# 906 more elements of a value block kept in PSUM, gate weights in two loads, one score product moved: a decode kernel that streams 218 MB

## The chip, the cores and the metric

The kernel runs on one core of a Trainium2 chip. The metric is the device time of one execution in microseconds (us). The profile's span, from the first to the last instruction, is about 1.4 us shorter than that time.

Engines are named as in the profile: PE is TensorE, PEld its weight loads, DVE VectorE, ACT ScalarE, POOL GpSimd, SP SyncE. SP issues nearly all loads, in one queue; 16 DMA engines carry them out. A "packet" is one row of one load as the trace records it: a load for 128 partitions has 128 packets, 8 for each DMA engine, and each packet has a start, a duration and a size.

## The reference, cut to what matters

One token goes twice through an attention layer and a gated MLP, with the same weights and the same caches both times.

```python
def _A_ref(x, k_cache, v_cache, wq, wo):      # 32 heads of 192, window of the last 4096 keys
    q = (x @ wq).reshape(B, Sq, Hq, Dh).transpose(0, 2, 1, 3)
    k = k_cache[:, :, Sk - W:, :]; v = v_cache[:, :, Sk - W:, :]
    p = softmax(einsum("bhqd,bhkd->bhqk", q, k) * Dh ** -0.5)
    return einsum("bhqk,bhkd->bhqd", p, v).transpose(...).reshape(B, Sq, Hq * Dh) @ wo

def _B_ref(x, w_gate, w_up, w_down):          # 640 -> 1536 -> 640
    return (sigmoid(x @ w_gate) * (x @ w_up)) @ w_down

x = A_x
x = x + _A_ref(layernorm(x), ...);  x = x + _B_ref(layernorm(x), ...)     # layer 0
x = x + _A_ref(layernorm(x), ...);  x = x + _B_ref(layernorm(x), ...)     # layer 1
```

(Transposes and shapes are abbreviated.) Each number of a cache or weight is used once per layer, so the work is moving them. What layer 0 leaves on the chip need not be loaded again in layer 1.

## The kernel before: the parts that matter

The heads are handled as 16 pairs. A pair has an "a" block (query weights and keys) and a "b" block (values and output weights), each 14208 bf16 elements per partition; SBUF has seven such slots and one region of 12288 elements, `mreg`, in cells of `FW` = 640. Pairs 0, 14 and 15 stay in their slots from layer 0 to layer 1. While the MLP weights of layer 0 stream through `mreg`, part of pair 1's values waits in PSUM banks that nobody uses then. DVE copies it in, 32 bits at a time ("stow"), and out again in layer 1:

```python
NST = 3 * FW // 2
stash = [(bank[i][:, c:c + n].bitcast(U32), 2 * n)
         for i, c, n in ((3, 0, NST // 2), (6, 0, NST // 2), (7, DC, 512 - DC))]
NSV = sum(n for _, n in stash)                 # 960 + 960 + 1014 = 2934 bf16 elements
...
# loads of the MLP weights into mreg: name -> (first cell, first block, last block)
MW = {"wg0": (0, 0, 3), "wg1": (3, 3, 6), "wg2": (6, 6, 9), "wg3": (9, 9, 12), "u0": (12, 0, 2), "u1": (14, 2, 7),
      "d0": (0, 0, 3), "d1": (3, 3, 6), "u2": (6, 7, 10), "u3": (9, 10, 12), "d2": (11, 6, 9), "d3": (14, 9, 12)}
MAFTER = {"d0": ("wg0",), "d1": ("wg1",), "u2": ("wg2",), ...}      # a load waits for the products that free its cells
# loads of the rest of pair 1's values: name -> (first cell, last cell)
MV = {"v1": (17, len(rc)), "v0": (NSV // FW, 6), "v2": (6, 11), "v3": (11, 14), "v4": (14, 17)}
VAFTER = {"v1": "u1", "v0": "d1", "v2": "u3", "v3": "d2", "v4": "d3"}
```

Here "wg", "u" and "d" are gate, up and down weights. "The gate weights of layer 1" means the gate weights that are loaded in this stage, at the passage from layer 0 to layer 1. The attention of layer 1 starts so:

```python
mark("a14_0", Q(14, 0))                        # query of pair 14; mark() lets loads be issued
mark("QM", Q(PM, 1, 5))                        # PM = 1: query of pair 1
ln_sq(xi)
mark("a14_1", QK(14, 0, ks=(0,)))              # scores of pair 14
mark("a14_2", QK(14, 0, ks=(1, 2)))
...
soft(1, hook=lambda: Q(2, None))               # softmax statistics of pair 15
for i in (2, 0, 1):
    ...                                        # the three copies from PSUM back to mreg
expo(1)                                        # exponential of pair 15
QK(0, 0)                                       # scores of pair 0, which free a slot
soft(0, mid=lambda: PVmm(14, 0))
```

Of the kernel before, what the change touches and what calls it, by code (L numbers as in the profile page):

```python
# [8 lines left out]
U32 = mybir.dt.uint32  # L9
# [9 lines left out]
DC, FC = D // P, F // P  # L19
# [90 lines left out]
def decode_kernel(ctx: ExitStack, nc, cx: bass.AP, uc: bass.AP,  # L110
# [52 lines left out]
    bank += [o8_ps[:, 0:512], o8_ps[:, 512:1024]] + [ctx.enter_context(nc.psum_tensor(f"bank{i}", [P, 512], FP32)) for i in (6, 7)]  # L163
    qe, dmx, oT3 = bank[2][:, 0:P], bank[2][:, P:2 * P], bank[2][:, 2 * P:2 * P + 3]
    o8, yT = bank[4:6], bank[7]
    stash = [(bank[i][:, c:c + n].bitcast(U32), 2 * n) for i, c, n in ((3, 0, NST // 2), (6, 0, NST // 2), (7, DC, 512 - DC))]
    NSV = sum(n for _, n in stash)

    def words(v, out, in_):
        return v.tensor_scalar(out=out.bitcast(U32), in0=in_.bitcast(U32), scalar1=0, scalar2=None, op0=ALU.bitwise_or)  # L170
# [4 lines left out]
    def res(name):  # L175
        if name not in R:
# [4 lines left out]
    rval = [res(f"val{i}") for i in range(NSLOT)]  # L181
    rc = [res(f"cell{i}") for i in range(-(-ME // FW))]
    MW = {"wg0": (0, 0, 3), "wg1": (3, 3, 6), "wg2": (6, 6, 9), "wg3": (9, 9, 12), "u0": (12, 0, 2), "u1": (14, 2, 7),
          "d0": (0, 0, 3), "d1": (3, 3, 6), "u2": (6, 7, 10), "u3": (9, 10, 12), "d2": (11, 6, 9), "d3": (14, 9, 12)}
    MAFTER = {"d0": ("wg0",), "d1": ("wg1",), "u2": ("wg2",), "u3": ("wg3",), "d2": ("wg3", "u0"), "d3": ("u1",)}
    MV = {"v1": (17, len(rc)), "v0": (NSV // FW, 6), "v2": (6, 11), "v3": (11, 14), "v4": (14, 17)}
    VAFTER = {"v1": "u1", "v0": "d1", "v2": "u3", "v3": "d2", "v4": "d3"}

    PLACE = {s: i for i, s in enumerate((0, 3, 2, 1, 4, 5, 6))}

# [36 lines left out]
    def last_values(l, p):  # L227
        return [("b1", l, p), ("b0", l, p)]
    seq = [("a", 0, 0)] + [("c", 0, p) for p in range(1, 15)] + [("a", 0, 15), ("b", 0, 14)] + last_values(0, 15)
    seq += [("wol", 14), ("wol", 15)] + [(k,) for k in (*MW, "v1", "wq2", "v0", "v2", "v3", "v4", "wq3", "wom")] + [("a0", 1), ("a0", 2), ("a", 1, 3), ("b", 1, 2)]  # L230
    seq += [("b", 1, 3), ("a", 1, 4), ("b", 1, 4), ("a", 1, 5), ("a", 1, 6), ("b", 1, 5)]
    seq += [("c", 1, p) for p in range(7, 13)] + [("a", 1, 13), ("b", 1, 12)] + last_values(1, 13)
    seq += [("fg",), ("fu",), *(("fd", i) for i in range(len(WFIN)))]
# [18 lines left out]
    def try_load(it):  # L252
        k = it[0]
        if k == "c":
            l, p = it[1:]
            ss = A_SLOT[l][p], B_SLOT[l][p - 1]
            if any(x in busy for x in ss):
                return False
            busy.update(ss)
            first = min(ss, key=PLACE.get)  # L260
            assert abs(PLACE[ss[0]] - PLACE[ss[1]]) == 1 and first == ss[p % 2]
            pg.dma(q_dma(slot(first, 0, 2 * UNIT), uc[p]), f"c{l}{p % 2}", wr=[rslot[x] for x in ss])
            values_in(ss[1])
        elif k == "a":
            s = A_SLOT[it[1]][it[2]]
            if not take(s):
                return False
            o0 = WQE if it[1:] == (1, 3) else 0
            pg.dma(q_dma(slot(s, o0, UNIT - o0), a_in(it[2], o0)), f"c{it[1]}{it[2] % 2}" if it[1:] in ((0, 15), (1, 4), (1, 5), (1, 6), (1, 13)) else f"a{it[1]}_{it[2]}", wr=[rslot[s]])
        elif k == "b":  # L270
            s = B_SLOT[it[1]][it[2]]
            if not take(s):
                return False
            o0, n0 = WOE if it[1:] == (0, 14) else 0, len(pg.ops["dma"])
            pg.dma(q_dma(slot(s, o0, UNIT - o0), b_in(it[2], o0)), f"b{it[1]}_{it[2]}", wr=[rslot[s]])
            if it[1:] == (0, 14):
                ev_done["b14"] = list(pg.ops["dma"][n0]["deps"].items())
            values_in(s)
        elif k == "b1":
            s = B_SLOT[it[1]][it[2]]  # L280
            if not take(s):
                return False
            n, o1 = len(pg.ops["dma"]), UNIT if it[1] else VE
            pg.dma(q_dma(slot(s, NHALF, o1 - NHALF), b_in(it[2], NHALF, o1)), f"b1_{it[1]}", wr=[rslot[s]])
            ev_done["b1"] = list(pg.ops["dma"][n]["deps"].items())
        elif k == "b0":
            s = B_SLOT[it[1]][it[2]]
            pg.dma(q_dma(slot(s, 0, NHALF), b_in(it[2], 0, NHALF)), "bh0", wr=[res("bh0")], extra=ev_done["b1"])
        elif k == "a0":
            if f"a14_{it[1]}" not in ev_done:  # L290
                return False
            s = A_SLOT[1][2]
            o0, o1 = ((WQE, A0CUT), (A0CUT, UNIT))[it[1] - 1]
            pg.dma(q_dma(slot(s, o0, o1 - o0), a_in(2, o0, o1)), f"a0{it[1]}", wr=[res(f"a0{it[1]}")] + ([rslot[s]] if it[1] == 2 else []),
                   extra=[ev_done[f"a14_{it[1]}"]])
        elif k == "wol":
            s = B_SLOT[0][it[1]]
            o = wo_at(it[1])
            pg.dma(q_dma(slot(s, o, WOE), b_in(it[1], o, o + WOE)), f"wol{it[1]}", wr=[res(f"wol{it[1]}")], extra=ev_done["b1" if it[1] == 15 else "b14"])
        elif k in MW:  # L300
            if any("done_" + n not in ev_done for n in MAFTER.get(k, ())):
                return False
            c, f0, f1 = MW[k]
            src = {"w": wg_d, "u": wu_d, "d": wd_d}[k[0]]
            pg.dma(q_dma(mreg(c * FW, (f1 - f0) * FW), src[:, f0 * FW:f1 * FW]), k, wr=rc[c:c + f1 - f0])
        elif k in MV:
            if "done_" + VAFTER[k] not in ev_done:
                return False
            c0, c1 = MV[k]
            o0, o1 = max(c0 * FW, NSV), min(c1 * FW, ME)  # L310
            pg.dma(q_dma(mreg(o0, o1 - o0), b_in(PM, o0, o1)), k, wr=rc[c0:-(-o1 // FW)])
        elif k == "wq2":
            if "done_d0" not in ev_done:
                return False
            pg.dma(q_dma(mreg(0, WQE), a_in(2, 0, WQE)), k, wr=rc[0:WQE // FW])
        elif k == "wq3":
            if "a14_0" not in ev_done:
                return False
            pg.dma(q_dma(slot(A_SLOT[1][2], 0, WQE), a_in(3, 0, WQE)), k, wr=[res(k)], extra=[ev_done["a14_0"]])
        elif k == "wom":  # L320
            if "QM" not in ev_done:
                return False
            pg.dma(q_dma(slot(A_SLOT[1][PM], 0, WOE), b_in(PM, VE, UNIT)), "wom", wr=[res("wom")], extra=[ev_done["QM"]])
        elif k == "fg":
            pg.dma(q_dma(mreg(0, 12 * FW), wg_d), "fg", wr=rc)
        elif k == "fu":
            if not take(U_SLOT):
                return False
            pg.dma(q_dma(slot(U_SLOT, 0, 12 * FW), wu_d), "fu", wr=[rslot[U_SLOT]])
        else:  # L330
            if it[1] == 0 and not take(D_SLOT):
                return False
            c0, c1 = WFIN[it[1]]
            pg.dma(q_dma(slot(D_SLOT, c0 * D, (c1 - c0) * D), wdp(c0, c1)), f"wf{it[1]}", wr=[rslot[D_SLOT]] if it[1] == 0 else [])
        return True
# [55 lines left out]
    def attention(l, xi):  # L391
# [42 lines left out]
                release(sa)  # L434
            return ev

        def soft(x=0, hook=None, mid=None):
            sc_x = S[x]
            pg.op("dve", lambda v: v.reduce_max(out=mx, in_=sc_x[0][:], axis=AX.X), wr=[res("mx")], ex=sc_x[3:5])  # L439
            if hook is not None:  # L440
# [2 lines left out]
            if mid is not None:  # L443
                mid()
            pg.op("pe", lambda t: t.matmul(dmx[:, 0:P], lhsT=ones_f, rhs=diag[:], start=True, stop=True), rd=[res("diag"), res("ones")], ex=[rb[2]])  # L445
            pg.op("dve", lambda v: v.tensor_reduce(out=nb2, in_=dmx[:, 0:P].rearrange("p (a r) -> p r a", r=2), axis=AX.X, op=ALU.max, negate=True),  # L446
                  wr=[res("nb2")], ex=[rb[2]])
            pg.op("dve", lambda v: v.tensor_tensor_reduce(out=nbj, in0=nb2, in1=pm_s, scale=1.0, scalar=0.0, op0=ALU.mult, op1=ALU.add, accum_out=nbias),  # L448
                  rd=[res("nb2"), res("pm_s")], wr=[res("nbj"), res("nbias")], multi=True)

# [14 lines left out]
                  rd=[res("rowsum"), res("wsel")], wr=[res(f"rs2{z}")])  # L465

        def RS(z, bk=4):
            sm = bank[bk][:, 2 * DH:2 * DH + 2]
            pg.op("pe", lambda t: t.matmul(sm, lhsT=ones_f, rhs=rs2[z], start=True, stop=True), rd=[res(f"rs2{z}"), res("ones")], wr=[res("rsum")], ex=[rb[bk]])  # L469
            for h in range(2):  # L470
                rb[bk].last["dve"] = pg.op("dve", lambda v, h=h: v.reciprocal(out=Rn[z][64 * h:64 * h + 64], in_=sm[64 * h:64 * h + 64, h:h + 1]),  # L471
# [83 lines left out]
        def step(p, prev):  # L555
# [1 line left out]
                ev = PVn(prev - 1, 1 - prev % 2)  # L557
            Q(p, 0)
            QK(p, 0)
            soft(0)  # L560
            if (l, prev) == (0, PM):
                stow(2, [ev])
            expo()
# [13 lines left out]
        def loop(p0, n):  # L577
            for it in range(n // 2):
                pg.seg = (l, it)
                for p in (p0 + 2 * it, p0 + 2 * it + 1):  # L580
                    step(p + 1, p)
                    if (l, p) == (0, PM):
                        stow(0)
                        stow(1)
            pg.seg = None
        if l == 0:
            Q(0, 0)
# [14 lines left out]
        else:  # L602
            mark("a14_0", Q(14, 0))
            mark("QM", Q(PM, 1, 5))
            ln_sq(xi)
            mark("a14_1", QK(14, 0, ks=(0,)))
            mark("a14_2", QK(14, 0, ks=(1, 2)))
# [4 lines left out]
            expo()  # L612
            ET(0)
            Q(0, 0)
            soft(1, hook=lambda: Q(2, None))
            for i in (2, 0, 1):
                o, n = sum(m for _, m in stash[:i]), stash[i][1]
                pg.op("dve", lambda v, i=i, o=o, n=n: words(v, mreg(o, n), stash[i][0]), rd=[res(f"stash{i}")], wr=rc[o // FW:-(-(o + n) // FW)],
                      ex=[rb[7]] if i == 2 else [], own="st")
            expo(1)  # L620
            QK(0, 0)
            soft(0, mid=lambda: PVmm(14, 0))
            PVout(14, 0)
            ET(1)
# [30 lines left out]
    def mlp(l, xi):  # L655
# [65 lines left out]
        for i in range(2):  # L721
            f0, f1 = HS[i], HS[i + 1]
            if i:
# [2 lines left out]
            pg.op("dve", lambda v, i=i, f0=f0, f1=f1: v.scalar_tensor_tensor(out=hT[:, f0:f1], in0=bank[ubank[i]][:, 0:f1 - f0], scalar=rstd_c,  # L726
                                                                            in1=eg[:, f0:f1], op0=ALU.mult, op1=ALU.mult),
                  rd=[res("rstd"), res("eg")], wr=[res(f"hT{i}")], ex=[rb[ubank[i]]])
        down("d2", "d3")
        return residual(xi)  # L730

    def finish():
# [213 lines left out]
```

## Time and profile before

| | before |
|---|---|
| time, median of 3 | 514.11 us (513.99 to 514.98) |
| span of the profiled execution | 512.7 us |
| bytes moved, mean rate | 218.71 MB, 427 GB/s |
| packet times of all queues, sum / 16 engines | 509.65 us |
| first packet, last landing of weights | 1.0 us, 510.2 us |

The first lines of the profile page of the kernel before: busy time and share for each engine, then slices (40 equal ones; a digit is a busy share in tenths), the rate in GB/s by slice, all packets, and the shares of the chain of waits that ended last.

```profile
span 512.7 us, 8580 instructions
...
PE 260.9 (51%) x3716; PEld 136.9 (27%) x3716; DVE 100.4 (20%) x379; ACT 84.8 (17%) x171; POOL 4.2 (1%) x31
...
DMA  9999999999999999999999999999999999999996
GB/s 426 430 423 426 427 430 428 426 435 448 439 430 426 440 430 430 426 435 457 399 422 416 418 440 436 435 430 427 443 443 443 430 426 426 440 431 417 431 427 275
DMA packets 9820, 218.71 MB, mean 427 GB/s; under 512 B 1224, under 2 KB 1608, under 8 KB 4808
...
DMA 63%; PE 23%; DVE 7%; ACT 3%; issue 2%; SPq 2%; DVEq 0%; POOL 0%; ACTq 0%; POOLq 0%
```

The row to read is DMA: 9 up to the last slice. No other engine is busy more than 51% of the time. The chain of waits gives DMA only 63%, which could tempt one to shorten the other 37%. But the chain follows one thread of waits through a steady flow; it doesn't say that the DMA engines rested while PE computed, and the DMA row says that they didn't, as far as slices of 12.8 us can. (A packet counts whole in the slice in which it starts. So single slices can show more than the mean rate, and shares in windows more than 1.)

How much the queue holds in reserve can be worked out: for each load, the last of its 16 completions in the trace, less the moment at which the next load is issued. I call this the *lead*. In the kernel before the smallest is 4.5 us. The 16 engines don't finish a load together (2 us apart in this stage), so the earliest engine's lead is smaller: the first of the 16 completions less the next issue, 2.5 us at least in this stage and 2.4 in the whole run.

The issue of loads between the layers, from SP's part of the timeline (start, duration, line, what is loaded, how many merged into the line):

```profile
259.99 1.86 SPq L214 DMA_DIRECT2D big<-in_wg_dram  x4
261.89 4.56 SPq L214 DMA_DIRECT2D big<-in_wu_dram  x2
275.25 0.90 SPq L214 DMA_DIRECT2D big<-in_wd_dram  x2
276.97 1.48 SPq L214 DMA_DIRECT2D big<-in_wu_dram  x2
```

The gate and up loads are in the queue 14 us ahead. From 275.25 us on, each load needs cells that the products have only just freed: here the queue is short.

The order of events around pair 0's scores (timeline; PE's scores L429, the copies out of PSUM L170, pair 15's exponential L453, and the next load):

```profile
301.29 2.75 PE L429 MATMUL scores<-big,qs 128*32 128x512 bf16 x24
...
301.83 1.94 DVE L170 TENSOR_SCALAR big<-bank 128x507 uint32<-128x507 uint32 x3
301.93 1.20 ACT L453 ACTIVATE e_sb<-o,sc 128x1024 bf16<-128x1024 f32 x1 [1.41 <-DVE sc L448]
...
304.09 0.33 SPq L214 DMA_DIRECT2D big<-in_uc_dram  x1
```

### The profile page before, as it was taken

The numbers are of one execution on the slowest core, as the hardware profiler recorded it, in microseconds if no ns is written. First come the engines' busy times: TensorE is split into PE (matmuls) and PEld (weight loads), VectorE is DVE, ScalarE is ACT, GpSimd is POOL, SyncE is SP. The second block draws the span as 40 slices with busy tenths as digits, with TensorE's granted clock in tenths as the row PEclk, the third lists the DMA queues.
The fourth block names the chain that finished last, engine by engine and source line by source line (L and its number), as shares of the span: only waits on it lengthen the run. The fifth ranks groups of instructions, "written<-read, shape, count | busy, mean of one in ns | idle before, by whom it ended". The sixth has DMA issues, their size and how long they took to land.

```text
span 512.7 us, 8580 instructions
## 1 busy us (share of the span) xinstructions
PE 260.9 (51%) x3716; PEld 136.9 (27%) x3716; DVE 100.4 (20%) x379; ACT 84.8 (17%) x171; POOL 4.2 (1%) x31
## 2 busy tenths in 40 slices
PE   0452456344634454326566767873625244634665
PEld 0221222122312221112234434432312122312334
DVE  0221221111210221112121243321202111210311
ACT  1110111011101111011121033130301011101220
POOL 0010000000000000000000000000000000000000
PEclk9995555566556566675575578665857556556675
DMA  9999999999999999999999999999999999999996
GB/s 426 430 423 426 427 430 428 426 435 448 439 430 426 440 430 430 426 435 457 399 422 416 418 440 436 435 430 427 443 443 443 430 426 426 440 431 417 431 427 275
DMA packets 9820, 218.71 MB, mean 427 GB/s; under 512 B 1224, under 2 KB 1608, under 8 KB 4808
## 3 DMA queue, kind: packets, MB, share of 16 engines
q1 hardware_dynamic: 9656, 218.37, 99.2%
q8 instruction: 13, 0.21, 0.1%
q10 hardware_dynamic: 144, 0.06, 0.0%
q14 instruction: 7, 0.06, 0.0%
HBM read 218.43 MB, written 0.00 MB: 426 GB/s over the span
## 4 chain that ended last, share of the span: by engine, by line
DMA 63%; PE 23%; DVE 7%; ACT 3%; issue 2%; SPq 2%; DVEq 0%; POOL 0%; ACTq 0%; POOLq 0%
DMA big<-in_uc_dram 54%; PE scores L429 9%; PE o L488 7%; DMA big<-in_wd_dram 6%; DMA big<-in_wu_dram 3%; DVE sc L439 3%; PE bank L445 2%; PE bank L411 2%; SPq L214 2%; ACT e_sb L453 2%; PE bank L523 1%; PE bank L459 1%; ACT diag L442 1%; DVE sc L471 1%; PE o L469 1%
## 5 line engine op out<-in xcount | busy, mean ns | idle before, releaser
L429 PE MATMUL scores<-big,qs 128*32 128x512 bf16 x744 | 83.6, 619 | 10.3 <-DVE qs L417 9.6
L411 PE MATMUL bank<-sh,big 128*128 128x1 bf16 x465 | 17.2, 166 | 133.3 <-DMA big<-in_uc_dram 130.9
L488 PE MATMUL o<-big,et_sb 128*2 128x384 bf16 x1024 | 76.1, 465 | 6.1 <-DMA big<-in_uc_dram 3.6
L442 ACT ACTIVATE diag<-cst,sc 128x128 f32<-128x128 bf16 x32 | 12.8, 401 | 310.2 <-DVE sc L439 299.3
L439 DVE TENSOR_REDUCE sc<-scores 128x1 f32<-128x1024 f32 x31 | 37.9, 1224 | 79.1 <-PE scores L429 79.1
L411 PEld LDWEIGHTS bank<-sh,big 128*128 128x128 bf16 x465 | 14.7, 104 | 136.5 <-DMA big<-in_uc_dram 113.2
L445 PE MATMUL bank<-diag,sc 128*128 128x128 f32 x64 | 21.8, 436 | 46.7 <-ACT diag L442 46.7
L453 ACT ACTIVATE e_sb<-scores,sc 128x1024 bf16<-128x1024 f32 x31 | 37.3, 1204 | 39.7 <-DVE sc L448 37.4
L417 DVE TENSOR_TENSOR qs<-bank,cst 128x96 bf16<-128x96 f32 x30 | 7.7, 258 | 163.6 <-PE bank L411 163.6
L488 PEld LDWEIGHTS o<-big,et_sb 128*2 128x2 bf16 x1024 | 27.8, 106 | 41.7 <-issue 28.6
L429 PEld LDWEIGHTS scores<-big,qs 128*32 128x32 bf16 x744 | 24.2, 134 | 45.0 <-issue 33.2
L495 ACT CAST o_sb<-o 128x384 bf16<-128x384 f32 x64 | 29.6, 474 | 21.4 <-PE o L488 21.3
L445 PEld LDWEIGHTS bank<-diag,sc 128*128 128x128 f32 x64 | 13.6, 265 | 71.5 <-ACT diag L442 70.5
L523 PE MATMUL bank<-sh,big 128*128 128x1 bf16 x480 | 17.3, 165 | 15.5 <-DVE sh L512 14.9
L463 DVE CAST et_sb<-bank 128x64 bf16<-128x64 f32 x32 | 7.2, 225 | 69.8 <-PE bank L459 69.8
L523 PEld LDWEIGHTS bank<-sh,big 128*128 128x128 bf16 x480 | 14.6, 99 | 18.0 <-DVE sh L512 12.4
L446 DVE TENSOR_REDUCE sc<-bank 128x2 f32<-128x128 f32 x32 | 9.3, 292 | 40.1 <-PE bank L445 40.1
L459 PE MATMUL bank<-cst,e_sb 128*128 128x8 bf16 x256 | 11.7, 169 | 7.8 <-ACT e_sb L453 7.6
L459 PEld LDWEIGHTS bank<-cst,e_sb 128*128 128x128 bf16 x256 | 9.0, 101 | 23.9 <-issue 17.4
L469 PE MATMUL o<-sc 128*128 128x2 f32 x62 | 13.8, 292 | 0.6 <-ACT o_sb L495 0.6
L469 PEld LDWEIGHTS o<-sc 128*128 128x128 f32 x62 | 11.9, 239 | 1.9 <-ACT o_sb L495 1.3
L471 DVE RECIPROCAL sc<-o 64x1 f32<-64x1 f32 x62 | 10.2, 164 | 10.0 <-PE o L469 8.2
(78 smaller groups left out, 105.9 us busy)
## 6 DMA issues: line engine op xcount, KB each, us to landing
big<-in_uc_dram SPq DMA_DIRECT2D x20, 7104.0 KB, 22.7
big<-in_uc_dram SPq DMA_DIRECT2D x11, 3552.0 KB, 21.4
big<-in_uc_dram SPq DMA_DIRECT2D x2, 3072.0 KB, 18.8
big<-in_uc_dram SPq DMA_DIRECT2D x7, 480.0 KB, 6.5
big<-in_uc_dram SPq DMA_DIRECT2D x1, 2784.0 KB, 12.3
big<-in_uc_dram SPq DMA_DIRECT2D x1, 2304.0 KB, 10.0
big<-in_uc_dram SPq DMA_DIRECT2D x1, 2048.0 KB, 11.7
big<-in_wg_dram SPq DMA_DIRECT2D x4, 480.0 KB, 15.1
```

The costliest lines, as they stand in the source:

```text
L411: ins = t.matmul(qe[:, i:i + 1], lhsT=w[:, c * 2 * DH + c0:c * 2 * DH + c0 + P], rhs=xq[:, c:c + 1], start=(c == 0), stop=(c == DC - 1))
L429: ins = t.matmul(sc_x[1 + b][32 * j:32 * j + 32, :], lhsT=qs[:, y, k, :], rhs=slot(sa, WQE + k * W + (4 * b + j) * 512, 512), start=(k == ...
L439: pg.op("dve", lambda v: v.reduce_max(out=mx, in_=sc_x[0][:], axis=AX.X), wr=[res("mx")], ex=sc_x[3:5])
L442: pg.op("act", lambda a: a.mul(out=diag[:], in_=ident, mul=mx), rd=[res("cst"), res("mx")], wr=[res("diag")])
L445: pg.op("pe", lambda t: t.matmul(dmx[:, 0:P], lhsT=ones_f, rhs=diag[:], start=True, stop=True), rd=[res("diag"), res("ones")], ex=[rb[2]])
L453: pg.op("act", lambda a: a.activation(out=e_sb[:], in_=sc_x[0][:], func=ACT.Exp, bias=nbias, scale=srs_c, accum_out=rowsum), rd=[res("nbia ...
L459: ins = t.matmul(qe[:, 0:2 * NB].rearrange("p (r x) -> p r x", r=2)[:, :, 4 * b:4 * b + 4], lhsT=e_sb[:, b * P:(b + 1) * P], rhs=sel, star ...
L469: pg.op("pe", lambda t: t.matmul(sm, lhsT=ones_f, rhs=rs2[z], start=True, stop=True), rd=[res(f"rs2{z}"), res("ones")], wr=[res("rsum")], ...
L471: rb[bk].last["dve"] = pg.op("dve", lambda v, h=h: v.reciprocal(out=Rn[z][64 * h:64 * h + 64], in_=sm[64 * h:64 * h + 64, h:h + 1]), rd=[r ...
L488: ins = t.matmul(o8[h][32 * j:32 * j + 2, 0:2 * DH].rearrange("p (a d) -> p a d", a=2), lhsT=et_sb[:, z, h * NB + 2 * u:h * NB + 2 * u + 2 ...
L495: pg.op("act", lambda a, h=h: a.copy(out=o8_sb[:, :, h * DH:(h + 1) * DH], in_=o8[h][:, 0:2 * DH].rearrange("p (a d) -> p a d", a=2)), wr= ...
L523: ins = t.matmul(yT[:, j:j + 1], lhsT=wo[:, c * D + j * P:c * D + (j + 1) * P], rhs=oTb[z][:, c:c + 1], start=False, stop=(c == 2), skip_g ...
```

## The change

The intent: fewer bytes (906 elements x 128 partitions x 2 bytes = 0.232 MB less), fewer packets for the gates, and an order in which the added copies don't hold up the loads. The core of the diff, with cuts marked:

```diff
-    stash = [... for i, c, n in ((3, 0, NST // 2), (6, 0, NST // 2), (7, DC, 512 - DC))]
+    SB = [(3, 0, NST // 2), (6, 0, NST // 2), (7, DC, 512 - DC), (2, 264, 248), (4, 2 * DH + 2, 126), (5, 2 * DH, 79)]
+    stash = [... for i, c, n in SB]
+    assert NSV == 6 * FW
...
-          ... "d2": (11, 6, 9), "d3": (14, 9, 12)}
+          ... "d2": (11, 6, 9), "d3": (14, 9, 11), "d4": (16, 11, 12)}
+    MD = {"wg0": (0, 0, 6), "wg2": (6, 6, 12), **{k: v for k, v in MW.items() if k[0] != "w"}}
-    MV = {"v1": (17, len(rc)), "v0": (NSV // FW, 6), "v2": (6, 11), ...}
-    VAFTER = {"v1": "u1", "v0": "d1", "v2": "u3", "v3": "d2", "v4": "d3"}
+    MV = {"v1": (17, len(rc)), "v0": (6, 9), "v2": (9, 11), ...}
+    VAFTER = {"v1": "u1", "v0": "u2", "v2": "u3", "v3": "d2", "v4": "d4"}
...                                                    # layer 0: where the copies into PSUM are made
-            soft(0)
+            soft(0, late=(lambda: stow(3)) if (l, prev) == (0, PM) else None)
...
-                        stow(0)
-                        stow(1)
+                        for i in (0, 1, 4, 5):
+                            stow(i)
...                                                    # layer 1
             mark("QM", Q(PM, 1, 5))
+            for i in (3, 4, 5):
+                unstow(i)
             ln_sq(xi)
...
-            soft(1, hook=lambda: Q(2, None))
+            soft(1, hook=lambda: (Q(2, None), QK(0, 0)))
             for i in (2, 0, 1):
-                ...
+                unstow(i)
             expo(1)
-            QK(0, 0)
             soft(0, mid=lambda: PVmm(14, 0))
...
-        down("d2", "d3")
+        down("d2", "d3", "d4")
```

The three further pieces lie in banks that are busy between the two layers' attention or during it, in columns that those uses leave alone (in bank 2, sums of two columns moved from column 384 to 260 to make room).

More of the change, by code (lines that the diff above doesn't have):

```diff
@@ L165, in decode_kernel @@
     o8, yT = bank[4:6], bank[7]
-    stash = [(bank[i][:, c:c + n].bitcast(U32), 2 * n) for i, c, n in ((3, 0, NST // 2), (6, 0, NST // 2), (7, DC, 512 - DC))]
+    SB = [(3, 0, NST // 2), (6, 0, NST // 2), (7, DC, 512 - DC), (2, 264, 248), (4, 2 * DH + 2, 126), (5, 2 * DH, 79)]
+    stash = [(bank[i][:, c:c + n].bitcast(U32), 2 * n) for i, c, n in SB]
     NSV = sum(n for _, n in stash)
+    assert NSV == 6 * FW
     def words(v, out, in_):
@@ L183, in decode_kernel @@
     MW = {"wg0": (0, 0, 3), "wg1": (3, 3, 6), "wg2": (6, 6, 9), "wg3": (9, 9, 12), "u0": (12, 0, 2), "u1": (14, 2, 7),
-          "d0": (0, 0, 3), "d1": (3, 3, 6), "u2": (6, 7, 10), "u3": (9, 10, 12), "d2": (11, 6, 9), "d3": (14, 9, 12)}
-    MAFTER = {"d0": ("wg0",), "d1": ("wg1",), "u2": ("wg2",), "u3": ("wg3",), "d2": ("wg3", "u0"), "d3": ("u1",)}
-    MV = {"v1": (17, len(rc)), "v0": (NSV // FW, 6), "v2": (6, 11), "v3": (11, 14), "v4": (14, 17)}
-    VAFTER = {"v1": "u1", "v0": "d1", "v2": "u3", "v3": "d2", "v4": "d3"}
+          "d0": (0, 0, 3), "d1": (3, 3, 6), "u2": (6, 7, 10), "u3": (9, 10, 12), "d2": (11, 6, 9), "d3": (14, 9, 11), "d4": (16, 11, 12)}
+    MD = {"wg0": (0, 0, 6), "wg2": (6, 6, 12), **{k: v for k, v in MW.items() if k[0] != "w"}}
+    MAFTER = {"d0": ("wg0",), "d1": ("wg1",), "u2": ("wg2",), "u3": ("wg3",), "d2": ("wg3", "u0"), "d3": ("u1",), "d4": ("u1",)}
+    MV = {"v1": (17, len(rc)), "v0": (6, 9), "v2": (9, 11), "v3": (11, 14), "v4": (14, 17)}
+    VAFTER = {"v1": "u1", "v0": "u2", "v2": "u3", "v3": "d2", "v4": "d4"}
     PLACE = {s: i for i, s in enumerate((0, 3, 2, 1, 4, 5, 6))}
@@ L229, in decode_kernel @@
     seq = [("a", 0, 0)] + [("c", 0, p) for p in range(1, 15)] + [("a", 0, 15), ("b", 0, 14)] + last_values(0, 15)
-    seq += [("wol", 14), ("wol", 15)] + [(k,) for k in (*MW, "v1", "wq2", "v0", "v2", "v3", "v4", "wq3", "wom")] + [("a0", 1), ("a0", 2), ("a", 1, 3), ("b", 1, 2)]
+    seq += [("wol", 14), ("wol", 15)] + [(k,) for k in (*MD, "v1", "wq2", "v0", "v2", "v3", "v4", "wq3", "wom")] + [("a0", 1), ("a0", 2), ("a", 1, 3), ("b", 1, 2)]
     seq += [("b", 1, 3), ("a", 1, 4), ("b", 1, 4), ("a", 1, 5), ("a", 1, 6), ("b", 1, 5)]
@@ L299, in try_load @@
             pg.dma(q_dma(slot(s, o, WOE), b_in(it[1], o, o + WOE)), f"wol{it[1]}", wr=[res(f"wol{it[1]}")], extra=ev_done["b1" if it[1] == 15 else "b14"])
-        elif k in MW:
+        elif k in MD:
             if any("done_" + n not in ev_done for n in MAFTER.get(k, ())):
                 return False
-            c, f0, f1 = MW[k]
+            c, f0, f1 = MD[k]
             src = {"w": wg_d, "u": wu_d, "d": wd_d}[k[0]]
@@ L435, in QK, with soft @@
             return ev
-        def soft(x=0, hook=None, mid=None):
+        def soft(x=0, hook=None, mid=None, late=None):
             sc_x = S[x]
@@ L447, in soft @@
                   wr=[res("nb2")], ex=[rb[2]])
+            if late is not None:
+                late()
             pg.op("dve", lambda v: v.tensor_tensor_reduce(out=nbj, in0=nb2, in1=pm_s, scale=1.0, scalar=0.0, op0=ALU.mult, op1=ALU.add, accum_out=nbias),
@@ L467, in RS @@
         def RS(z, bk=4):
-            sm = bank[bk][:, 2 * DH:2 * DH + 2]
+            so = 260 if bk == 2 else 2 * DH
+            sm = bank[bk][:, so:so + 2]
             pg.op("pe", lambda t: t.matmul(sm, lhsT=ones_f, rhs=rs2[z], start=True, stop=True), rd=[res(f"rs2{z}"), res("ones")], wr=[res("rsum")], ex=[rb[bk]])
@@ L604, in attention, with unstow @@
             mark("QM", Q(PM, 1, 5))
+            def unstow(i):
+                o, n = sum(m for _, m in stash[:i]), stash[i][1]
+                pg.op("dve", lambda v: words(v, mreg(o, n), stash[i][0]), rd=[res(f"stash{i}")], wr=rc[o // FW:-(-(o + n) // FW)],
+                      ex=[rb[SB[i][0]]], own="st")
+            for i in (3, 4, 5):
+                unstow(i)
             ln_sq(xi)
@@ L614, in attention @@
             Q(0, 0)
-            soft(1, hook=lambda: Q(2, None))
+            soft(1, hook=lambda: (Q(2, None), QK(0, 0)))
             for i in (2, 0, 1):
-                o, n = sum(m for _, m in stash[:i]), stash[i][1]
-                pg.op("dve", lambda v, i=i, o=o, n=n: words(v, mreg(o, n), stash[i][0]), rd=[res(f"stash{i}")], wr=rc[o // FW:-(-(o + n) // FW)],
-                      ex=[rb[7]] if i == 2 else [], own="st")
+                unstow(i)
             expo(1)
-            QK(0, 0)
             soft(0, mid=lambda: PVmm(14, 0))
```

## The prediction

> **What bounds the kernel now.** The DMA engines. The page's slices give the DMA row as 9 in 39 of 40; PE is busy 51%, DVE 20%, ACT 17%. 218.71 MB at 427 GB/s are 512 us of the 512.7 us span. The trace's DMA packets add up to 509.6 us for each of 16 engines, between the first at 1.0 us and the last landing of weights at 510.2 us: no gap. The Trainium skill, "DMA: Bandwidth & Descriptors", section "Where 436 GB/s comes from", puts the fabric ceiling at 435 GB/s; this trace agrees. The chain of waits alternates compute and DMA only because loads are issued when a buffer comes free; each is issued at least 4.5 us before the previous one has landed. So only fewer bytes, cheaper packets, or a queue that runs dry can move the time.
>
> **What the change does to the queue (packet means of this trace, 8 packets per engine and load).**
> - 906 elements less of pair 1: loads with rows of 1812 and 6400 B (75 + 244 ns) become 3840 and 2560 B (149 + 102): -68 ns x 8 = -0.54 us. By bytes, 0.232 MB at 427 GB/s is the same.
> - Gate weights: four packets of 149 ns become two of 291: -14 x 8 = -0.11 us, and two completions less.
> - Last down weights in two loads: 149 becomes 102 + 55: +0.06 us, one completion more (9 ns).
> Sum about -0.6 us, all on the critical path because the queue never rests.
>
> **What it adds and moves elsewhere, estimated from this trace.**
> - Three more copies into PSUM in layer 0, three out in layer 1. Copies of 480 and 507 words took 652 and 685 ns, so 248, 126 and 79 words should take 0.37, 0.22 and 0.17 us. The first hides under pair 0's value products (2.7 us); the others delay the load that waits for them (issued at 57.5 us, backlog 5.2) by 0.4 us. Free. Those of layer 1 fall under the 2.75 us of pair 14's scores: free.
> - Gate halves: the first products start when 6 blocks are there, so the first down load is issued at 275.8 instead of 275.3 (backlog 4.3 instead of 4.9). The first of pair 1's values waits for the third up load, 1.2 us later; still over 4 us. The engines' completions lie 2 us apart there, so the earliest engine keeps about 2.3.
> - Last down product of layer 0: 5 matmuls instead of 15 after the last landing, attention starts 0.3 us earlier.
> - Pair 0's scores begin at about 299.5 instead of 301.3; the load behind them is issued at 302.3 instead of 304.1; pair 15's exponential moves from 301.9 to about 303.6, later value products slip by 1.5 us. The backlog there is 7 to 18 us: no effect.
>
> **Prediction.** 513.5 us, 80% range 512.9 to 514.2. Faster by over 2%: 1%; within 2%: 98%; slower by over 2%: 1%.
>
> **What would show it right or wrong.** DMA total 218.48 MB, mean rate unchanged at 427, DMA row 9 throughout, packet sum per engine and last weight landing both 0.6 us less; the tail after it (2.5 us) unchanged; each load still issued 4 us before the previous landing.
>
> **What would make it wrong.** The load queue waiting in the weight stage (275 to 295 us) until an engine runs dry: a DMA share under 0.9 in 4 us there; the new vector order around 300 us reaching a load with little backlog; instruction fetches falling on another engine, shifting the last landing by tenths of a us; and spread as large as the effect (513.99 to 514.98).

## The result, and the profile after

| | before | after |
|---|---|---|
| time, median of 6 | 514.05 us (513.75 to 514.98) | 513.76 us (513.40 to 514.35) |
| ratio, 95% interval | | 0.9992 (0.998 to 1.0005) |
| span of the profiled execution | 512.7 us | 512.2 us |
| bytes | 218.71 MB | 218.47 MB |
| load queue: packet times / 16 | 508.39 us | 507.97 us |
| the same with each packet at the median of its size | 506.80 us | 506.20 us |
| packet excess at 255 to 300 us (see below) | 0.10 us | 0.63 us |
| last completion of weights | 510.24 us | 509.78 us |
| smallest lead after the gates | 4.5 us | 4.4 us |

Ratios here and below are the mean time of one kernel's runs over that of the other's of the same rounds, so not quite the ratio of the medians that are quoted. Executions over 1.5% slower than the fastest of the same kernel are left out of the means. The difference by the ratio is 0.4 us, and its interval reaches 1, so by this table alone the gain isn't established (run e1 adds to it).

The page of the changed kernel, the same lines:

```profile
span 512.2 us, 8583 instructions
...
PE 262.5 (51%) x3716; PEld 138.4 (27%) x3716; DVE 101.5 (20%) x385; ACT 85.1 (17%) x171; POOL 4.3 (1%) x31
...
DMA  9999999999999999999999999999999999999996
GB/s 426 426 427 426 427 430 428 430 453 444 426 430 430 431 435 426 430 448 444 399 420 412 409 440 434 432 430 427 450 439 435 430 430 439 431 431 413 434 424 280
DMA packets 9676, 218.47 MB, mean 427 GB/s; under 512 B 1208, under 2 KB 1592, under 8 KB 4664
...
DMA 64%; PE 22%; DVE 8%; ACT 3%; issue 2%; SPq 1%; DVEq 0%; POOL 0%; ACTq 0%; POOLq 0%
```

Same rate, same full DMA row, 0.24 MB less. The issue of loads of the changed kernel between the layers:

```profile
259.49 0.91 SPq L217 DMA_DIRECT2D big<-in_wg_dram  x2
260.44 0.91 SPq L217 DMA_DIRECT2D big<-in_wu_dram  x2
275.45 0.80 SPq L217 DMA_DIRECT2D big<-in_wd_dram  x2
277.74 0.81 SPq L217 DMA_DIRECT2D big<-in_wu_dram  x2
```

The first down load is issued at 275.45 us, 0.2 us later than before, while the up load ahead of it landed 0.4 us earlier; its lead fell from 4.93 to 4.36 us. The further up loads lost more, from 5.55 to 4.42.

The copies, in the view of their source line (minimum, median and maximum in ns), into PSUM and out of it:

```profile
L172 DVE TENSOR_SCALAR bank<-big x4: 409/649/683, 52.4 to 56.5; 128x480 uint32<-128x480 uint32 x2, 128x248 uint32<-128x248 uint32 x1, 128x507 uint32<-128x507 uint32 x1
L172 DVE TENSOR_SCALAR o<-big x2: 230/255/280, 57.0 to 57.2; 128x126 uint32<-128x126 uint32 x1, 128x79 uint32<-128x79 uint32 x1
L172 DVE TENSOR_SCALAR big<-bank x4: 407/652/682, 289.2 to 305.7; 128x480 uint32<-128x480 uint32 x2, 128x248 uint32<-128x248 uint32 x1, 128x507 uint32<-128x507 uint32 x1
L172 DVE TENSOR_SCALAR big<-o x2: 241/266/292, 289.6 to 290.0; 128x126 uint32<-128x126 uint32 x1, 128x79 uint32<-128x79 uint32 x1
```

The three new ones took 0.41, 0.28 and 0.23 us into PSUM where 0.37, 0.22 and 0.17 were estimated. And the new order around pair 0's scores, whose 2.75 us now begin 3.8 us before the copies (0.5 us before the change):

```profile
300.70 2.75 PE L432 MATMUL scores<-big,qs 128*32 128x512 bf16 x24
...
304.45 1.94 DVE L172 TENSOR_SCALAR big<-bank 128x507 uint32<-128x507 uint32 x3
...
304.57 1.20 ACT L458 ACTIVATE e_sb<-o,sc 128x1024 bf16<-128x1024 f32 x1 [2.86 <-DVE sc L453]
```

The scores begin at 300.70 us (before 301.29), the load behind them is issued at 303.50 (before 304.09), and the exponential slips from 301.93 to 304.57. The prediction had each of these 1.0 to 1.2 us earlier: in this execution pair 15's scores took 2.75 us where the trace of before has 1.48, and the granted clock at 292 to 296 us was 0.50 where it was 0.89.

One thing isn't as predicted. With each packet at its median for its size, the sum fell by exactly the predicted 0.60 us; the measured sum fell by 0.42. I call *packet excess* the sum, over all packets of the load queue that start in a stretch, of the time above the median for their size in that execution, divided by 16. Over the whole run it rose by 0.18 us, which is the difference; between 255 and 300 us alone it rose from 0.10 to 0.63 us, and it fell by 0.35 us elsewhere, mostly before that stretch. Near 280.3 us some 3840-byte packets of the loads behind the first down load, 149 ns as a rule, took up to 1566 ns. (An instruction packet of 16384 bytes started at 280.30 us too. One at 279.90 us in the kernel before came without such packets, but a part of the excess may be due to that meeting.) The same place in 4 us windows (PE, PEld, DVE, ACT and POOL busy, granted clock, DMA share, GB/s), first before, then after:

```profile
276.00:280.00 4.00, 1.81 (x42) 1.65 (x42) 0.40 (x2) 0.73 (x3) 0.00 (x0) 0.50 1.04 426
280.00:284.00 4.00, 2.18 (x64) 1.97 (x65) 0.23 (x1) 0.00 (x0) 0.00 (x0) 0.50 1.02 410
```

```profile
276.00:280.00 4.00, 1.80 (x47) 1.72 (x48) 0.40 (x2) 0.73 (x3) 0.00 (x0) 0.50 1.01 413
280.00:284.00 4.00, 2.33 (x70) 2.03 (x68) 0.23 (x1) 0.00 (x0) 0.00 (x0) 0.50 1.02 380
```

In the second window the rate drops to 380 GB/s although the DMA share stays at 1.02: the engines are marked busy with packets that take too long. A DMA share alone hides this.

### The profile page after: what moved, and what is told of

The parts are those of the page before. It is cut to its first block, busy times and chain, and to the rows that moved or that the text cites. A ratio compares the mean times of both kernels' runs of the same rounds, so it can differ in the third digit from the quotient of the medians.

```text
span 512.2 us, 8583 instructions
## 1 busy us (share of the span) xinstructions
PE 262.5 (51%) x3716; PEld 138.4 (27%) x3716; DVE 101.5 (20%) x385; ACT 85.1 (17%) x171; POOL 4.3 (1%) x31
## 2 busy tenths in 40 slices
DMA packets 9676, 218.47 MB, mean 427 GB/s; under 512 B 1208, under 2 KB 1592, under 8 KB 4664
## 4 chain that ended last, share of the span: by engine, by line
DMA 64%; PE 22%; DVE 8%; ACT 3%; issue 2%; SPq 1%; DVEq 0%; POOL 0%; ACTq 0%; POOLq 0%
DMA big<-in_uc_dram 54%; PE scores L432 8%; DMA big<-in_wd_dram 6%; PE o L494 6%; DMA big<-in_wu_dram 4%; DVE sc L442 3%; PE bank L448 2%; ACT e_sb L458 2%; PE bank L414 2%; PE bank L529 1%; SPq L217 1%; PE bank L464 1%; ACT diag L445 1%; DVE sc L477 1%; DVE qs L420 1%
## 5 line engine op out<-in xcount | busy, mean ns | idle before, releaser
L432 PE MATMUL scores<-big,qs 128*32 128x512 bf16 x744 | 82.0, 608 | 10.3 <-DVE qs L420 9.6
L494 PE MATMUL o<-big,et_sb 128*2 128x384 bf16 x1024 | 77.4, 471 | 8.5 <-DMA big<-in_uc_dram 4.2
```

What stands on the lines that cost most here:

```text
L432: ins = t.matmul(sc_x[1 + b][32 * j:32 * j + 32, :], lhsT=qs[:, y, k, :], rhs=slot(sa, WQE + k * W + (4 * b + j) * 512, 512), start=(k == ...
L494: ins = t.matmul(o8[h][32 * j:32 * j + 2, 0:2 * DH].rearrange("p (a d) -> p a d", a=2), lhsT=et_sb[:, z, h * NB + 2 * u:h * NB + 2 * u + 2 ...
```

## The experiments

Theory at the outset: the load queue never rests, so the change is worth what its packets save, and nothing else in it matters. Rivals: the gain comes from the changed order; or the layer transition is bound by waits, so bytes are hidden; or there is no gain at all, only noise. All kernels gave the correct result. Runs 1 to 8 shared one chip and runs 9 to 12 another, each group with its own runs of the kernel before. The excess is from the one profiled execution of each kernel; for the kernel before it is 0.10, for the changed kernel's first trace 0.63.

| run | edit to the changed kernel | median us | mean | ratio to before (95%) | packets at median / 16 | excess 255 to 300 us |
|---|---|---|---|---|---|---|
| e1 | none | 513.73 | 513.78 | 0.9991 (0.9977 to 1.0005) | 506.20 | 0.48 |
| e2 | 906 elements loaded again | 514.16 | 514.27 | 1.0003 (0.9989 to 1.0016) | 506.74 | 0.28 |
| e3 | nothing in PSUM | 515.94 | 516.00 | 1.0034 (1.0020 to 1.0047) | 508.54 | 0.57 |
| e4 | gates in 12 loads | 514.22 | 514.15 | 0.9997 (0.9984 to 1.0011) | 506.91 | 0.16 |
| e5 | gates in 1 load | 515.43 | 515.23 | 1.0019 (1.0005 to 1.0033) | 506.12 | 1.45 |
| e6 | gates in 4 loads | 513.63 | 513.71 | 0.9991 (0.9978 to 1.0003) | 506.33 | 0.10 |
| e7 | scores in the old place | 513.67 | 513.76 | 0.9988 (0.9975 to 1.0002) | 506.20 | 0.55 |
| e8 | copies out three times | 514.73 | 514.76 | 1.0014 (0.9999 to 1.0029) | 506.20 | 0.29 |
| e9 | gates in 4 loads, 226 more elements kept | 513.43 | 513.55 | 0.9990 (0.9977 to 1.0003) | 506.20 | 0.37 |
| e10 | last down weights in 1 load | 513.95 | 513.84 | 0.9995 (0.9982 to 1.0008) | 506.13 | 0.37 |
| e11 | two long DVE instructions | 513.78 | 514.01 | 0.9998 (0.9986 to 1.0011) | 506.20 | 0.15 |
| e12 | twelve tiny DVE instructions | 513.68 | 513.68 | 0.9992 (0.9979 to 1.0004) | 506.20 | 0.14 |

e5's mean leaves out its slow run of 540.49 us (its median includes it).

### e1: the changed kernel again

> The changed kernel once more, to put its small gain on more runs. Main theory (the DMA queue never rests, so only the packets' time counts): 0.4 to 0.6 us under the kernel before. Rival (nothing but noise): 0.0. Rival (the gain is from the moved scores and the shorter last products): any value, but then the run without the move shows it.

Ratio 0.9991, or 0.46 us. Two independent sets give 0.4 and 0.46 us, in the expected range, each with an interval that includes no gain. Put together, the 11 runs of the changed kernel have a mean of 513.79 us and the 16 of the kernel before 514.16: a gain of 0.37 us, 95% interval 0.06 to 0.68, which no longer includes none. The following runs show with larger doses where it comes from. Differences between the means of two single runs below are uncertain by 0.5 us or more either way.

### e2 and e3: the bytes, undone and in four times the dose

```diff
-    SB = [..., (7, DC, 512 - DC), (2, 264, 248), (4, 2 * DH + 2, 126), (5, 2 * DH, 79)]
+    SB = [..., (7, DC, 512 - DC)]                            # e2; and "v0": (NSV // FW, 9)
```

> The changed kernel with the old three PSUM pieces: 906 elements of pair 1 are loaded again, in the first of its loads (rows of 5652 B for 3840 B); gate halves, the split down load and the moved scores stay. Main theory: 906 x 256 B at 427 GB/s are 0.54 us, so the time is 0.54 us over the changed kernel, about equal to the kernel before. Rival (the gain is from the order): as fast as the changed kernel, 0.4 us under the kernel before.

```diff
-    ... ("a", 1, 3), ("b", 1, 2)]
+    ... ("a", 1, 3), ("vl",), ("b", 1, 2)]                   # e3: "vl" loads mreg(0, 3840); no stow, no unstow
```

> The changed kernel with nothing at rest in PSUM: all copies gone, 3840 more elements (0.98 MB) loaded in one load in layer 1. Four times the dose of the change. Main theory: rows of 7680 B, 8 packets of 291 ns per engine, so 2.3 us over the changed kernel and 1.8 over the kernel before. Rival (the layer transition is bound by waits, where removing six vector copies helps and bytes are hidden): under 1 us over the changed kernel.

By the means, e2 is 0.49 us over e1 (expected 0.54), not clear of noise by itself, and e3 2.22 us over e1 (expected 2.3). e3's interval lies clear of 1 even against the kernel before. The two agree with a response in proportion to the bytes: 2.22 us for 3840 elements is 0.52 for 906. (e3 also leaves out the copies and adds one load.) Its 2.22 us are far above the "under 1 us" of the rival in which waits hide the bytes. The page of e3 shows the added bytes and an unchanged DMA row:

```profile
DMA  9999999999999999999999999999999999999996
...
DMA packets 9820, 219.46 MB, mean 426 GB/s; under 512 B 1224, under 2 KB 1608, under 8 KB 4808
```

### e4, e5 and e6: the gate weights in twelve, one and four loads

```diff
-    MD = {"wg0": (0, 0, 6), "wg2": (6, 6, 12), **{...}}
+    MD = {**{f"wg{i}": (i, i, i + 1) for i in range(12)}, **{...}}     # e4
+    MD = {"wg0": (0, 0, 12), **{...}}                                  # e5
+    MD = MW                                                            # e6
```

> The changed kernel with the gate weights of layer 1 in twelve loads of one block (rows of 1280 B) in place of two. Main theory: 12 packets of 55 ns for 2 of 291 are +78 ns x 8 = 0.62 us, and ten completions of about 9 ns are 0.09: 0.7 us over the changed kernel, though the first products may start earlier. Rival (the number of loads matters through the time at which the products start): equal or faster than the changed kernel, because products follow the data more closely.

> The changed kernel with all gate weights of layer 1 in one load (rows of 15360 B). Packets alone: 573 ns for 2 of 291, -9 ns x 8 = 0.07 us less. But the first product must wait for all 12 blocks, so the first down load should be issued near 277.8 us instead of 275.5, when the load before it is about 2 us from landing: the 16 engines land 2 us apart, so the earliest should run dry for about 1 us and the latest not at all. Theory A (the engine that ends last sets the time): 0.0 to 0.2 us over the changed kernel. Theory B (any idle engine costs in proportion): 0.5 us or more.

> The changed kernel with the gate weights of layer 1 in the old four loads. Main theory: four packets of 149 ns for two of 291 are 14 ns x 8 and two completions, 0.13 us over the changed kernel. Below what five rounds resolve in time; the sum of packet times should show it. Rival (larger loads start the products later and so cost): faster than the changed kernel.

At their medians the packets cost what was said: twelve loads 0.71 us more, four loads 0.13 more, one load 0.08 less. By the means, twelve loads were 0.37 us over e1 and four loads 0.07 under it; neither can be told from what the packets say. One load, the cheapest in packets, was 1.45 us slower (0.6 us or more with the noise), and that is clear: at this dose a second term works against the large gate load.

Its first down load had to wait for all gates and was issued at 277.71 us, with a lead of 2.1 us to the latest engine and 0.2 us to the earliest. The DMA row of e5's page and, below it, the windows to set beside the four lines above:

```profile
DMA  9999999999999999999999999999999999999996
...
276.00:280.00 4.00, 2.61 (x78) 2.54 (x79) 0.00 (x0) 0.60 (x3) 0.00 (x0) 0.50 0.81 282
280.00:284.00 4.00, 1.78 (x55) 1.53 (x52) 0.63 (x3) 0.14 (x1) 0.00 (x0) 0.50 0.96 317
```

The load's first packet started at 278.66 us, 0.95 us after the issue, and first packets took 459 to 1138 ns in place of 149 (an instruction packet that started at 278.46 us may have its part in this). The latest completions lost time too: two loads of 3840 bytes a row, 1.2 us each as a rule, moved the latest one from 279.79 to 282.93 us. Expectation A, that only the engine that ends last counts and that it loses nothing, gave 0.0 to 0.2 us and was wrong; the measured loss fits B, half a microsecond or more. The page's DMA row reads 9 here as everywhere: a queue that ran dry for about a microsecond doesn't show in it.

e6 undoes this part of the change alone, and its time can't be told from that of the changed kernel. Its windows in its one trace:

```profile
276.00:280.00 4.00, 1.90 (x45) 1.73 (x46) 0.40 (x2) 0.73 (x3) 0.00 (x0) 0.50 1.03 422
280.00:284.00 4.00, 2.33 (x70) 2.09 (x70) 0.23 (x1) 0.00 (x0) 0.00 (x0) 0.50 1.01 407
```

The first down load of e6 was issued with a lead of 4.92 us, as before the change, and the excess is back at 0.10. After these runs it seemed that gate halves cost the excess and four loads don't; e9 and e10 put that to the test.

### e7: the scores in their old place

```diff
-            soft(1, hook=lambda: (Q(2, None), QK(0, 0)))
+            soft(1, hook=lambda: Q(2, None))
...
             expo(1)
+            QK(0, 0)
```

> The changed kernel with pair 0's scores in their old place, after the copies out of PSUM and pair 15's exponential. Main theory: the load behind the scores is issued 1 to 2 us elsewhere with 7 us of backlog, so the time is that of the changed kernel within 0.1 us. Rival (the gain of the change is from this move): 0.4 us slower than the changed kernel, equal to the kernel before.

Mean 513.76 us, e1 513.78. The load behind the scores was issued at 304.32 us instead of 303.50, with 6.5 us of lead. e7 is 0.40 us under the 16 runs of the kernel before (interval 0.08 to 0.73), so it keeps the gain without the new order. The reordering isn't the source of the gain, and nothing here shows that it costs anything either.

### e8, e11 and e12: how much delay the order can take

```diff
-            for i in (3, 4, 5):
+            for i in (3, 4, 5) * 3:                          # e8; and (2, 0, 1) * 3
...
+            pg.op("dve", lambda v: v.reduce_max(out=sc[:, 13:14], in_=cst[:, 0:1].to_broadcast([P, 1400]), axis=AX.X), ...)   # e11, 3800 in the second place
...
+            for i in range(6): pg.op("dve", lambda v: v.memset(sc[:, 13:14], 0.0), ...)                                       # e12, in both places
```

> The changed kernel with each of the six copies out of PSUM done three times (same result): 1.5 us more VectorE work before pair 14's softmax and 4 us more before pair 0's. Main theory: the loads that are issued after it have 6 to 16 us of backlog, so the time is unchanged within 0.2 us. Rival (the copies stand on the critical path, and the change pays for them with part of its 0.6 us): 4 to 5 us slower.

e8 fits neither number. Its five times are 514.06, 515.58, 513.72, 514.73 and 515.70 us: some like the changed kernel, some 2 us slower, 1.0 us slower on average. Far from 4 to 5 us, but not nothing. The next two runs separate the delay from the number of instructions.

> The run with three times the copies was 1 us slower on average, though its profiled execution was not. This one adds about the same VectorE time in the same two places (1.5 and 4 us) with two instructions instead of twelve. If the time of the delay is what costs (in some executions a load comes too late): about 1 us slower than the changed kernel, with as wide a spread (512 to 514 in span). If the number of instructions costs: as fast as the changed kernel.

> The other half of that question: twelve tiny instructions in the same two places, under 1 us of VectorE time in all. If the time of the delay costs: as fast as the changed kernel. If the number of instructions costs (their fetch): 1 us slower.

e12 is as fast as the changed kernel, within 0.25 us from run to run: twelve more instructions don't cost. e11's two instructions took 1.60 and 4.10 us; five of its six times lie at 513.3 to 514.2 us and one at 515.54. The expected 1 us on average isn't there (0.2), the wide spread is. Its trace shows how the delay arrives at the queue. A load that was issued at 310.46 us in the changed kernel, in e8's trace at 313.28, is issued here at 315.02:

```profile
315.02 0.33 SPq L217 DMA_DIRECT2D big<-in_uc_dram  x1
```

Its lead is 3.3 us to the latest engine and 1.5 us to the earliest (9.1 and 6.3 in the changed kernel), and at its start packets took too long again. The windows at that place, changed kernel and then e11:

```profile
316.00:320.00 4.00, 2.76 (x57) 1.87 (x58) 2.35 (x9) 1.87 (x4) 0.09 (x1) 1.00 1.02 440
320.00:324.00 4.00, 3.10 (x47) 1.72 (x51) 0.52 (x3) 0.67 (x2) 0.00 (x0) 0.59 0.99 423
```

```profile
316.00:320.00 4.00, 4.00 (x52) 1.59 (x48) 0.36 (x2) 1.84 (x4) 0.09 (x1) 0.50 1.03 402
320.00:324.00 4.00, 3.37 (x67) 1.81 (x59) 1.68 (x4) 0.51 (x2) 0.00 (x0) 0.83 0.92 391
```

The packet excess between 300 and 400 us is 1.13 us in e11, 0.22 in the changed kernel and in e8. So 5.7 us of DVE time brought a lead of 9.1 us down to 3.3, and what remained was too thin. The slow ones of e8's runs may be executions in which its lead of 6.4 us was shorter, but its profiled execution was a fast one, so this isn't shown; nor is why e8 was slow in three of five runs and e11, with as much delay, in one of six.

### e9 and e10: a better version, and one more trace with gate halves

```diff
-    SB = [(3, 0, NST // 2), (6, 0, NST // 2), ..., (5, 2 * DH, 79)]
+    SB = [(3, 0, 512), (6, 0, 512), ..., (5, 2 * DH, 128)]                        # e9; and MD = MW
-    ... "d3": (14, 9, 11), "d4": (16, 11, 12)}
+    ... "d3": (14, 9, 12)}                                                        # e10
```

> The changed kernel with the gate weights in the old four loads (as in the run before that had this alone) and 226 further elements of pair 1 at rest: the PSUM pieces of banks 3, 6 and 5 widened from 480, 480 and 79 words to 512, 512 and 128. Packet times: against the kernel before, -0.54 for the 906 elements, +0.07 for the split down load, -0.14 for the 226 elements: 0.6 us less by packets. Theory from the traces (the gate halves made the queue thin, and packets of the next loads took 0.3 to 0.5 us longer; four loads avoid that): packet excess in the weight stage near 0.1 us, time 0.6 to 0.7 us under the kernel before, so about 0.2 under the changed kernel. Rival (halves save their 0.13 us): 0.0 to 0.1 under the changed kernel.

> The changed kernel with the last three blocks of down weights in one load again; gate halves stay. By packets 0.07 us less than the changed kernel, not to be resolved in time: 513.3 to 513.9 us. For the theory of the thin queue it is one more trace with gate halves: packet excess in the weight stage 0.3 to 0.6 us, as in the other kernels with halves, where the kernels with four or twelve gate loads had 0.1 to 0.2. If it shows 0.1, the excess isn't bound to the halves.

e9 has the lowest median and mean of all kernels run, 513.43 and 513.55 us, and the lowest bytes, 218.42 MB; its ratio of 0.9990 is 0.5 us under the kernel before. The interval still touches 1, and the step from the changed kernel to e9 (0.2 us) can't be told from noise. Its excess was 0.37, not the expected 0.1.

e10's excess was 0.37, inside the expected 0.3 to 0.6, and e11 and e12, which have gate halves too, showed 0.15 and 0.14. Over all traces the kernels with halves have 0.14 to 0.63 us (nine traces, mean 0.38), those with four or twelve gate loads 0.10 to 0.37 (four traces, mean 0.18). The ranges overlap. That a much thinner queue costs is shown, by e5 and at another place by e11. That the halves, which shorten the lead of the first down load by half a microsecond and that of the up load after the two down loads by 1.1 us, cost 0.2 us is consistent with it, but the sums of the stage don't settle it.

Two other figures go further. The first is a load's loss by completions: the mean of its 16 completions, less that of the load before, less eight packets at their median. For the second down load and the up load after it together it is 0.09 to 0.10 us in all four traces with four or twelve gate loads, where that up load had a lead of 5.5 to 5.7 us. It is 0.10 to 0.34 us, 0.21 on average, in the nine with halves, where the lead was 4.3 to 5.0. (About 0.09 us of each is the instruction packet near 280 us and the packet after it.) The second is the time less the packets at their median: 7.56 us as the mean of 36 runs of seven kernels with halves (the changed kernel, e1, e2, e3, e7, e10, e12), 7.35 us of 38 runs with four gate loads (the kernel before, e6, e9). The difference, 0.22 us before rounding (interval 0.07 to 0.37), is clear of zero, and its middle lies above the 0.13 us that the halves save in packets. It pools kernels that differ in other ways, and two chips, so it is a comparison and not an experiment. Why packets lengthen at such a lead stays open; the meeting with the instruction packet isn't excluded.

## Why the prediction was right

- **What bounds the kernel: right.** DMA row 9 throughout in both, 427 GB/s in both, close to the 433 GB/s of 16 engines at the rate of the largest packets (56832 bytes in 2098 ns). The time follows the bytes: +2.22 us for 3840 elements, against 2.3 expected.
- **The bytes, -0.54 us: right.** By packets at their medians 506.74 in e2 against 506.20; by time 0.49 us, within its noise, and 0.52 us in proportion to e3.
- **Gate halves, -0.11 us and two completions: right in packets, not found in time.** At their medians the packets saved 0.13 us (e6 against e1), but e6 wasn't slower. This is the mis-sized term of the sum: "Gate weights: four packets of 149 ns become two of 291: -14 x 8 = -0.11 us". In time e6 against e1 puts it at +0.07 us, with noise of 0.5; the pooled comparison above puts it at about +0.1 (-0.13 in packets, +0.22 beside them). The prediction had named the risk ("The load queue waiting in the weight stage (275 to 295 us) until an engine runs dry") and set it aside for the first down load, because 4.3 us of backlog were left and about 2.3 for the earliest engine. Both leads came out as said (4.36 and 2.45 us). It had not looked at the up load after the two down loads, whose lead fell from 5.55 to 4.42 us and at which about half of the loss lies, and it had taken the lead as either enough or not. What the traces show in its place: packets lengthen while the DMA share stays at 1.0.
- **Last down weights in two loads, +0.06 us: consistent.** 0.07 us by packets (506.13 in e10); not to be resolved in time.
- **Copies free: right at their size.** The load that waits for the copies in layer 0 was issued at 57.47 us against 57.51 before, with 5.1 us of lead. The delay of 0.4 us that was expected is made up because the two copies of 480 words began 0.37 us earlier (55.90 against 56.27). The doses of e8 and e11 show that the reserve isn't unlimited.
- **Attention of layer 1 earlier by 0.3 us: 0.6 us in the trace.** Pair 14's scores began at 289.02 us against 289.61.
- **Order of the scores without effect: right** (e7), with the single times of the stage up to 1.2 us off.
- **Sum.** Predicted 513.5 us from 514.11; measured 513.76. By the ratios the gain is 0.4 and 0.46 us instead of 0.6, and 0.37 (0.06 to 0.68) with all runs together. The missing 0.2 us is as large as the loss of the halves, but the runs of these two kernels alone don't resolve it. That the number came within 0.3 us of the measured one owes something to luck: three runs of the kernel before had a spread of 1 us. The tail after the last completion stayed: 512.7 - 510.2 = 2.5 us before, 512.2 - 509.8 = 2.4 after.

## What to carry to other kernels

When the DMA row is full from end to end, cost a change by adding up packet times from the trace (count x median for the size / engines) and ask of everything else how far it shortens the lead of the load queue, for each load that it delays. The chain of waits gave 37% to other things than DMA here, but moving a score product (e7) changed nothing that could be measured. Merging loads saves packet time but delays everything that waits for the first part, so it can thin the queue elsewhere: compute the lead to the earliest and to the latest engine before and after. A gain of a tenth of a percent is best shown twice: that it exists, by all runs together, and where it comes from, by a larger dose of the same cause.

## What the Trainium skill lacked or had wrong

- "DMA: Bandwidth & Descriptors", Specifications, gives about 0.6 us to the first byte for loads issued from SP. e5 agrees, counted from the end of the issue: it began at 277.71 us, took 0.33, and the first packet started at 278.66, 0.62 us later. The kernel before starts alike: issue from 0.00 to 0.39 us, first packet at 1.01. What that section lacks is that the first packets then took longer, 459 to 1138 ns in place of 149 in e5 and up to 1.98 us in place of 1.05 at the start of the kernel before, so the start-up of a queue that has run thin costs more than that latency.
- No page gives the lead that a load stream needs. Here a lead of 0.2 us to the earliest engine (e5) gave an excess of 0.50 us on the load concerned and 1.5 us (e11) one of 0.44; at 2.4 us and more it was mostly under 0.1, with single cases to 0.23 in the changed kernel. But loads behind a thin one suffer too: packets that started from 281.6 to 283.0 us in e5, where its third load was due, which was issued with 3.3 us, had an excess of 0.64 us.
- "DMA: Bandwidth & Descriptors", Measured (HBM→SBUF, 128 partitions, SWDGE, issued from GpSimd), has the rule to batch loads to 1 MiB or more for 75% of peak. For a queue that stays full, issued from SP, it is too strict: rows of 1280 bytes (loads of 160 KB) took 55 ns, 23.3 bytes per ns, against 27.1 for rows of 56832 bytes (2098 ns), so 86% of the best rate (84% with the 9 ns of a completion).
- No page says how many loads SP can have under way. An issue mostly takes 0.33 to 0.43 us, but with nine loads not yet landed it took 2.06 and 2.46 us in the kernel before and 2.60 and 2.46 us in e4. It cost nothing that shows: the lead was 10 to 15 us at these issues.
- "Runtime: NRT & Kernel Launch", Instruction fetch mechanics, calls the cost of crossing a 16 KiB block of instructions mostly hidden. Whether it is for the engines that compute was not looked at here; for the load stream it isn't free: 13 packets of 16384 bytes of instructions took 0.88 to 0.96 us each in the kernel before, and 11 of them were followed, as they ended, by a load packet 0.4 to 0.6 us longer than its median. The instruction packets alone are 0.75 us of 16 engines' time.
